# Float32 e of heads 2 to 7 in seven shared buffers, fewer whole chunks, v split in two passes, first loads in parts: an attention and feed-forward kernel

## The chip, the cores and the metric

The kernel runs on one core of a Trainium2 chip. The metric is the device time of one execution in microseconds (us). The engines are TensorE (PE in the rows, its weight loads PEld), VectorE (DVE), ScalarE (ACT), GpSimd (POOL) and SyncE (SP), which here only issues DMAs.

## The reference

Attention over 4 batches of 8 heads, with the queries averaged in pairs, and behind it one feed-forward block on the joined heads:

```
B, H, S, D = q.shape                      # 4, 8, 1152, 64
q_pool = q.reshape(B, H, S // 2, 2, D).mean(axis=3)
scores = np.matmul(q_pool, k.transpose(0, 1, 3, 2)) / np.sqrt(D)
scores = scores - np.max(scores, axis=-1, keepdims=True)
attn = np.exp(scores)
attn = attn / (np.sum(attn, axis=-1, keepdims=True) + 1e-09)
x = np.matmul(attn, v)                    # heads joined: 2304 tokens of 512
h = x @ w_in                              # 512 -> 1024
e = np.exp(h - np.max(h, axis=-1, keepdims=True))
solu = h * e / (np.sum(e, axis=-1, keepdims=True) + 1e-09)
out = layer_norm(solu) * g_ln @ w_out     # 1024 -> 512
```

## The kernel before, in words

A *head* g is one of the 32 (batch, head) combinations, a *pair* P two heads next to each other. A head has 576 averaged queries and 1152 keys, and the keys are taken in nine *chunks* j of 128, so that the kernel has 288 chunks, numbered s = 9g + j. For a chunk, TensorE multiplies the keys (stationary) by the queries into a PSUM bank, ScalarE writes the exponential, and TensorE multiplies e (stationary, 128 queries at a time) by the chunk's v of 64 columns and a column of ones, whose sum is the softmax's denominator. The maxima that are subtracted come from a coarser product of the same operands (`maxima`, VectorE's reductions of `mx`), one head ahead.

Float32 precision is reached in one of two ways. In a *split* chunk ScalarE writes e twice, as float16 (`eh`) and as float32 (`e32`, printed `e`), and GpSimd (`rest`, L1119) writes their difference, again float16, behind the first in the same buffer; v is split alike into `vhi` and `vlo`; TensorE then makes 12 float16 multiplications of 64 or 65 columns per chunk. In a *whole* chunk (`whole`, `values_whole`) e is written once, in float32, and TensorE multiplies it with the float32 `vx`, in four multiplications per chunk (five in heads 0 and 1). `EX` in the table `KP` says which chunks are whole: half of chunks 10 to 70. For e in float32 there are two buffers.

`pair(P)` loads k, q and v of a pair and prepares them. For v: a sum of absolute values (`am`), the scale `vs`, v times the scale in place (`v_mul`, on ScalarE in pairs with "B" in `VM`, on VectorE in the others), the float16 part (`v_hi`, ScalarE) and the difference (`v_lo`, GpSimd). Pair 0 has a path of its own: k is transposed by TensorE (`k_tr0`), copied by ScalarE to `w` (`k_hi0`) with VectorE making the rest (`k_lo0`), q likewise (`q_tr`, `q_hi`, `q_lo`) after its pairs were added (`pool_q`) and the sum copied beside itself (`dup_q`); a DMA copies k's upper part once more (`k_again`, L1072). Fifteen reductions of 384 columns give head 0's maxima, which are joined, transposed (`turn0`) and written as a row of `q2` (`shift0`) before its first scores.

The feed-forward weights come as 64 bit numbers in 16 parts, eight of `w_in` and eight of `w_out`. Each part is unpacked (`weight_part`: two `up` on ScalarE, two multiplications on TensorE, L547 and a maximum on VectorE) and later scaled and split in two float16 parts (`weight_split`: L605 on ScalarE, one multiplication, one VectorE pass). 18 token tiles of 128 follow (`tokens`), the first of them during head 9.

The order is made when the program is built. `add` notes each step with its engine, an estimated length and a due time in chunks, to which the table `OFF` adds a number of its own for each step; `Plan.run` goes through an estimated course in which each engine takes the ready step with the earliest due time whose buffers are free. What results is a fixed order on each engine; on the chip each instruction then waits for its semaphores. `warm` fills TensorE's gaps in the first chunks with transposes that nobody reads (L1554). `tag` says how many buffers of a name there are and which names share them: `zw1`, `zw2`, `zq1`, `zq2` (pair 0's k and q), `e` (the tokens'), `ln` and `lt` share seven.

Of the kernel before, what the change touches and what calls it, by code (L numbers as in the profile page):

```python
# [42 lines left out]
class Plan:  # L43
# [77 lines left out]
    def run(self):  # L121
# [85 lines left out]
        while events:  # L207
# [129 lines left out]
def attention_solu_moe(  # L337
# [47 lines left out]
    banks = {"np0": [(4,), (5,), (6,), (0,), (1,), (2,), (3,)], "cp0": [(0, 1), (2, 3)], "av": [(7,)], "opx": [(7,)], "tpp": [(0, 1), (2, 3)]}  # L385
# [5 lines left out]
    banks["tpf"] = [(0,), (1,), (2,), (3,)]  # L391
# [112 lines left out]
    for t in w2h:  # L504
        nc.gpsimd.memset(t[D:D + 1, :], ONE)
# [3 lines left out]
    for t in qb:  # L509
        nc.gpsimd.memset(t, 0.0)  # L510
# [414 lines left out]
    def maxima(g, at, span):  # L925
# [109 lines left out]
        if not P:  # L1035
            return finish(a)
# [549 lines left out]
```

## Time and profile before

| | |
|---|---|
| median of 3 runs | 625.68 us (624.82 to 627.17) |
| the profiled execution | 629.79 us, of which its span on the core 628.0 us |
| mean granted clock of TensorE | 0.991 |
| busy: PE, DVE, ACT, POOL | 601.0, 517.9, 502.5, 476.7 us |
| share of the span | 96%, 82%, 80%, 76% |

PE's busy time counts a matmul from its issue to its modelled end. The matmuls overlap, so a busy PE is not one at its peak; the distance between starts says what a matmul costs.

### The profile page before, as it was taken

To read this page: it belongs to the slowest core of one execution; us is meant where nothing else is said; L and a number is where in the kernel's file an instruction comes from. 1 tells how busy PE (TensorE), PEld (TensorE's weight loads), DVE (VectorE), ACT (ScalarE), POOL (GpSimd) and SP (SyncE) were. 2 spreads that over 40 slices of the span, in tenths; PEclk is the share of its full clock that TensorE was granted. 3 is DMA by queue.
4 is the path that set the end of the run, shared out by engine and by line. 5 is a ranking of instruction groups with operands and counts; after the bars stand their busy time and mean duration, and the time that the engine had idled before them with its cause. 6 is when DMAs were issued, how large, how long until landed. Compare 5 with 4: busy or idle time off the path is not lost. (4 is left out here: it accounts for less than half of the span.)

```text
span 628.0 us, 17132 instructions
## 1 busy us (share of the span) xinstructions
PE 601.0 (96%) x6637; PEld 376.3 (60%) x6637; DVE 517.9 (82%) x1112; ACT 502.5 (80%) x950; POOL 476.7 (76%) x487
## 2 busy tenths in 40 slices
PE   7999999999988799999999999999999999999997
PEld 7877767567645356656555565566556666654443
DVE  4999889988999979899998889797899795638731
ACT  4488797999889688998898889898789897946531
POOL 5198454758689899999999998899898999941110
PEclk8989999999899999999999999999999999999999
DMA  9466969577836659495949575958777644044712
GB/s 240 91 106 197 224 179 237 141 184 145 159 92 123 155 98 168 115 179 122 172 85 187 130 129 116 172 149 122 139 155 150 114 72 61 19 94 85 135 34 50
DMA packets 183374, 83.59 MB, mean 133 GB/s; under 512 B 168572, under 2 KB 168572, under 8 KB 183292
## 3 DMA queue, kind: packets, MB, share of 16 engines
q1 hardware_dynamic: 183212, 82.36, 62.9%
q8 instruction: 52, 0.85, 0.6%
q14 instruction: 30, 0.25, 0.1%
q10 hardware_dynamic: 80, 0.13, 0.1%
HBM read 36.70 MB, written 4.72 MB: 66 GB/s over the span
## 5 line engine op out<-in xcount | busy, mean ns | idle before, releaser
L1119 POOL TENSOR_TENSOR eh<-e,eh 128x512 f16<-128x512 f32 (+1 forms) x268 | 318.3, 1206 | 39.4 <-ACT e L1098 15.4
L955 DVE TENSOR_REDUCE mx<-bank 128x1 f32<-128x512 f32 (+1 forms) x300 | 188.0, 652 | 19.3 <-PE bank L457 18.7
L1098 ACT ACTIVATE eh<-bank 128x512 f16<-128x512 f32 (+3 forms) x267 | 159.3, 623 | 23.8 <-PE bank L457 22.9
L1098 ACT ACTIVATE e<-bank 128x512 f32<-128x512 f32 (+1 forms) x257 | 156.2, 617 | 22.3 <-POOL eh L1119 17.0
L457 PEld LDWEIGHTS <-eh 128*128 128x128 f16 x3112 | 132.9, 99 | 59.8 <-issue 5.3
L457 PE MATMUL bank<-q,w 128*128 128x64 f16 (+2 forms) x612 | 140.1, 291 | 7.5 <-ACT r L1109 2.3
L457 PE MATMUL bank<-vhi,eh 128*128 128x65 f16 x2070 | 144.6, 195 | 2.4 <-ACT eh L1098 1.2
L457 PE MATMUL bank<-q,w2h 65*128 65x512 f16 (+1 forms) x540 | 126.9, 287 | 0.0
L457 PE MATMUL bank<-wb,xt 128*128 128x512 f16 x432 | 111.9, 379 | 2.4 <-ACT eh L1098 1.4
L457 PE MATMUL bank<-wb,lt 128*128 128x512 f16 x432 | 112.8, 379 | 0.4 <-DVE e L1325 0.4
L457 PE MATMUL bank<-w,q 128*128 128x512 f16 (+2 forms) x390 | 107.1, 335 | 1.8 <-DVE mx L955 1.2
L457 PE MATMUL bank<-vlo,eh 128*128 128x64 f16 x1042 | 98.4, 195 | 0.0
L457 PEld LDWEIGHTS <-w2h 65*128 65x128 f16 x540 | 45.4, 98 | 36.2 <-issue 16.4
L457 PEld LDWEIGHTS <-xt 128*128 128x128 f16 x432 | 38.7, 98 | 39.3 <-issue 3.0
L457 PEld LDWEIGHTS <-w 128*128 128x128 f16 x540 | 47.3, 99 | 22.1 <-issue 1.5
L1125 POOL TENSOR_TENSOR er<-r,er 128x320 f16<-128x320 f32 (+1 forms) x60 | 51.5, 860 | 8.4 <-ACT r L1109 4.0
L457 PEld LDWEIGHTS <-lt 128*128 128x128 f16 x432 | 38.0, 98 | 33.2 <-issue 0.9
L897 POOL TENSOR_TENSOR vlo<-vx,vhi 128x1152 f16<-128x1152 f32 x16 | 39.5, 2467 | 19.8 <-ACT vhi L893 19.8
L1358 POOL TENSOR_TENSOR st<-st 128x1 f32<-128x1 f32 x54 | 14.3, 266 | 49.4 <-ACT junk L1345 44.3
L457 PEld LDWEIGHTS <-q 128*128 128x128 f16 x360 | 30.8, 99 | 16.2 <-issue 0.9
L457 PEld LDWEIGHTS bank<-vx,eh 128*128 128x128 f32 x256 | 32.0, 190 | 3.3 <-DVE x L1201 1.4
L1318 ACT ACTIVATE e<-bank,st,xs 128x512 f32<-128x512 f32 x36 | 27.9, 778 | 7.5 <-DVE st L1311 7.5
(130 smaller groups left out, 923.9 us busy)
## 6 DMA issues: line engine op xcount, KB each, us to landing
qt<-in_q_dram SPq DMA_DIRECT2D x16, 576.0 KB
kt<-in_k_dram SPq DMA_DIRECT2D x32, 288.0 KB
vx<-in_v_dram SPq DMA_DIRECT2D x32, 288.0 KB
out_dram<-o SPq DMA_DIRECT2D x35, 128.0 KB
khi<-w SPq DMA_DIRECT2D x30, 144.0 KB
w2h<-w SPq DMA_DIRECT2D x30, 144.0 KB
raw<-in_moe_w_in_dram SPq DMA_DIRECT2D x8, 511.6 KB
raw<-in_moe_w_out_dram SPq DMA_DIRECT2D x8, 511.6 KB
```

The lines of the kernel that those rows point to most:

```text
L457: nc.tensor.matmul(out=o, lhsT=a, rhs=b, start=first, stop=last, skip_group_check=True)
L897: nc.gpsimd.tensor_tensor(out=o, in0=t, in1=h, op=ALU.subtract)
L955: nc.vector.tensor_reduce(out=tl["mx", g][:, m, c:c + 1], in_=tl["nps", (g, m, c)], op=ALU.max, axis=AXX)
L1098: nc.scalar.activation(out=o if P else o.rearrange("p (f i) -> p f i", f=2), in_=i, func=ACTF.Exp, scale=esc)
L1119: eng.tensor_tensor(out=e[:, o:o + c.stop - c.start], in0=e32[:, c], in1=e[:, c], op=ALU.subtract)
L1125: eng.tensor_tensor(out=e[:, :, 1, :], in0=tl["r32", (g, u)][:, 0:len(RU[u]), :], in1=e[:, :, 0, :], op=ALU.subtract)
L1318: nc.scalar.activation(out=tl[E][:, f * 512:(f + 1) * 512], in_=tl[H_[f]], func=ACTF.Exp, bias=st(2), scale=xs[:, r, 3:4], accum_out=st(3 ...
L1358: nc.gpsimd.tensor_tensor(out=st(o), in0=st(a), in1=nhalf if b is None else st(b), op=op)
```

## The change

*e in float32.* `place` gives `e32` of heads 2 to 7 (`ZE`) to the seven shared buffers, which heads 0 and 1 have left and the tokens don't use yet. Later heads keep two.

*Fewer whole chunks.* `EX` of chunks 10 to 70 goes from 50 to 33 of 100: 31 whole chunks become 20, three in head 1 (before four) and 17 in heads 2 to 7 (before 27). Counted in the order: 45 float32 multiplications by `vx` fewer, 134 float16 ones with `eh` and `vhi` or `vlo` more, ten more exponentials `e` of 512 columns, nine more GpSimd differences `eh` of 512 (VectorE makes two more).

*v in two passes from pair 4* (`VN`). ScalarE scales and rounds in one pass (`v_hi`), VectorE scales and subtracts in one (`v_lo`, L471). `v_mul` and GpSimd's pass are gone there: 12 GpSimd passes fewer, 12 VectorE passes of the new kind for eight `v_mul`, four `v_mul` of ScalarE fewer.

*Pair 0.* k of head 0 and q are loaded in thirds, in turn, and each third is worked on by itself. The copy beside the sum is gone: `q_hi` writes the two halves of `q1` in two passes, and VectorE alone adds. `k_again` of heads 0 and 1 is no DMA any more but a second ScalarE copy from PSUM (`k_hi0b`). Head 0's maxima are closed in two parts, for the first 384 queries and the rest, and its scores, exponentials and PSUM banks are in halves of 288 queries (`tpq`). GpSimd's constant fills are steps of the plan, after the first needed ones, and ScalarE's table is loaded by a copy in the preamble. `k_hi` of pair 1 is made by GpSimd (`KH`).

*Times anew.* All of `OFF` is new, and in `KP` the due times of the weight parts (`W`) and of their splitting (`WS`), which are later. Counted by the exponentials `eh` ahead of them in ScalarE's order: of the 32 `up`, 6 stand in heads 0 and 1 as before, 16 in heads 2 to 7 (before 24), 10 in heads 8 to 11 (before 2). `w_out` is split beside chunks 93 to 103 (before 78 to 88). The first token's exponential stands at chunk 88 in both.

```diff
+        if k[0] == "e32":
+            a, z = KP["ZE"]
+            return ("ze32", *k[1:]) if a <= k[1][0] < z else k
...
-    tag(KP["ZB"], "zw1", "zw2", "zq1", "zq2", "e", "ln", "lt")
+    tag(KP["ZB"], "zw1", "zw2", "zq1", "zq2", "ze32", "e", "ln", "lt")
...
+            for i in range(3):
+                add("SP", DMA(kb / 3), -60 + i, lambda i=i: load_k0(0, i), [], [("kt", 0, (0, i))])
+                add("SP", DMA(2 * kb / 3), -59.5 + i, lambda i=i: load_q(i), [], [("qt", 0, i)])
+            add("SP", DMA(kb), -50, lambda: load_k0(1), [], [("kt", 0, 1)])
...
+        def k_hi0b(i, h):
+            o = tl["w2", h][0:D, i * PW:(i + 1) * PW]
+            nc.scalar.copy(out=o, in_=flat(tl["kps", (h, i, 0)]))
...
+            if P in KP["KH"]:
+                add("POOL", POOL(2 * SQ), at, lambda: k_hi(1), [KT, S_], [(*KN, 0)])
...
+            for s in range(2):
+                nc.scalar.copy(
+                    out=tl["q1", P][D * s:D * s + D, :, 3 * i:3 * i + 3, :],
+                    in_=tl["qps", (P, i)].rearrange("p t h i -> p h t i"),
+                )
...
+            nc.scalar.activation(out=o, in_=i, func=ACTF.Copy, scale=tl["vs", P][:, 3:4])
...
+            left(o, t, tl["vs", P][:, 3:4], h)
...
+            if P >= KP["VN"]:
+                add("ACT", ACT(2 * SQ, 1, 1), at_v + 4.5, v_hi, [V, S], [H_])
+                add("DVE", 1326, at_v + 5, v_lo, [V, S, H_], [("vlo", P, 0)], port=1)
+                return
...
+        def finish(ats):
+            for f, at in enumerate(ats):
+                add("DVE", 83, at, lambda f=f: all0(f), [("mx", g, m, c) for m in range(5)[MZ[f]] for c in range(3)], [("mz", 0, f)])
+                add("PE", TR(3 - f), at, lambda f=f: turn0(f), [("mz", 0, f)], [("cp0", (g, f))], kind="whole")
+                add("DVE", DVE((384, 192)[f]), at, lambda f=f: shift0(f), [("cp0", (g, f))], [("q2", 0, "cd"[f], g)])
```

In `KP`, `EX` goes from [[10, 71, 50], [42, 282, 0]] to [[10, 71, 33], [42, 282, 0]], `W` from [2, 4.44, 37.52, 4.7] to [5, 5.2, 61, 4.1], `WS` from [47, 70, 0.22] to [54, 96, 0.22]; `ZE` [2, 8], `VN` 4 and `KH` [1] are new.

Three places of the order follow. The first is the start of SP's queue, before (`kt` and `qt` are k and q, `vx` is v, `raw` a weight part, `w` pair 0's k):

```order
L640 DMA qt<-in_q_dram 128x1152
L637 DMA kt<-in_k_dram 128x576 x2
L648 DMA vx_80<-in_v_dram 128x9x64 x2
L632 DMA kt<-in_k_dram 128x576 x2
L528 DMA raw<-in_moe_w_in_dram 128x4093
```

And with the change:

```order
L644 DMA kt<-in_k_dram 128x192
L650 DMA qt<-in_q_dram 128x384
L644 DMA kt<-in_k_dram 128x192
L650 DMA qt<-in_q_dram 128x384
L644 DMA kt<-in_k_dram 128x192
L650 DMA qt<-in_q_dram 128x384
L644 DMA kt<-in_k_dram 128x576
```

One load of q and one of k became six small ones, k's first third at the head; v moved behind them, the first weight part far back.

The second place is the start of ScalarE's order before (`q` is the transposed q, `am` the sum over v):

```order
L670 ACT_TABLE_LOAD
L670 COPY qt<-qt 128x3x64
L751 CAST w_173<-bank 64x384
L784 CAST q_178<-bank 128x2x192
L751 CAST w_173<-bank 64x384 x2
L784 CAST q_178<-bank 128x2x192 x2
L537 ACTIVATE up<-raw,ebias 128x512 x2
L854 ACTIVATE vlo,am<-vx_80 128x1152
```

And with the change (`w_138` is head 0's k, `w_132` its second copy, `w_203` and `w_186` the same of head 1):

```order
L503 ACT_TABLE_LOAD
L503 COPY ebias<-nhalf 128x1
L746 CAST w_138<-bank 64x384
L750 CAST w_132<-bank 64x384
L746 CAST w_138<-bank 64x384
L750 CAST w_132<-bank 64x384
L795 CAST q_164<-bank 64x2x192 x2
L746 CAST w_138<-bank 64x384
L750 CAST w_132<-bank 64x384
L795 CAST q_164<-bank 64x2x192 x4
L746 CAST w_203<-bank 64x384
```

The copy of `qt`, which stood first and read what GpSimd adds, is gone; the six casts of head 0 became twelve, and the weight unpacking `up` no longer stands among them.

The third place is VectorE's order at v of pair 5, before (`wb` weights, `qb` q's lower part, `mx` maxima, `st` a token's maximum):

```order
L955 TENSOR_REDUCE mx<-bank 128x1
L889 TENSOR_SCALAR vx_81<-vx_81,vs 128x18x64
L467 SCALAR_TENSOR_TENSOR wb_69<-wb_69,ws_73,bank 128x512
L467 SCALAR_TENSOR_TENSOR qb_84<-qt,qs,qa 128x9x64
L1183 COPY low_2860<-bank 64x65
```

And with the change:

```order
L553 SCALAR_TENSOR_TENSOR wb_69<-raw,bank 128x512
L471 SCALAR_TENSOR_TENSOR vlo<-vx_81,vs,vhi_83 128x1152
L1358 TENSOR_REDUCE st<-bank 128x1
L471 SCALAR_TENSOR_TENSOR qb_84<-qt,qs,qa 128x9x64
L559 TENSOR_REDUCE wm_71<-wb_69 128x1
```

VectorE's scaling in place became its pass to `vlo`, and the weight work beside it is unpacking now, where it was splitting.

## Rows read from the trace of the kernel before

**Rows 1.** Busy time of each engine in six stretches; then PEclk, DMA share, GB/s

```profile
0.00:26.30 26.30, 22.61 (x161) 21.71 (x162) 15.91 (x36) 7.97 (x15) 10.02 (x24) 0.94 0.76 186
34.00:49.00 15.00, 14.85 (x177) 11.71 (x176) 14.05 (x28) 11.84 (x22) 14.26 (x19) 0.93 0.79 148
69.00:159.50 90.50, 87.23 (x971) 61.88 (x970) 81.80 (x181) 79.78 (x150) 56.16 (x49) 1.00 0.77 189
159.50:232.00 72.50, 63.26 (x795) 38.46 (x794) 66.64 (x141) 60.76 (x117) 60.76 (x58) 0.98 0.59 122
232.00:557.00 325.00, 320.96 (x3996) 192.75 (x3995) 277.86 (x598) 286.19 (x554) 308.26 (x292) 1.00 0.65 128
557.00:628.00 71.00, 66.42 (x315) 30.91 (x313) 36.48 (x84) 30.98 (x56) 8.51 (x30) 0.99 0.39 77
```

**Rows 2.** Timeline of the first 34 us: start, duration, engine, instructions; in brackets idle before

```profile
0.72 0.40 SPq L640 DMA_DIRECT2D qt<-in_q_dram  x1
...
4.66 0.63 DVE L666 TENSOR_TENSOR qt<-qt 128x192 f32<-128x192 f32 x2 [4.66 <-DMA qt<-in_q_dram]
...
6.63 1.21 DVE L500 TENSOR_SCALAR idb<-ident 128x128 bf16<-128x128 f32 x2
...
9.58 0.35 ACT L670 COPY qt<-qt 128x192 f32<-128x192 f32 x1 [3.59 <-POOL qt L666]
9.84 0.47 ACT L751 CAST w<-bank 64x384 fp32r<-64x384 f32 x1
...
10.34 0.55 DVE L460 TENSOR_TENSOR w<-bank,w 64x384 fp32r<-64x384 f32 x1 [2.49 <-ACT w L751]
...
15.67 7.06 DVE L1010 TENSOR_REDUCE mx<-bank 128x1 f32<-128x384 f32 x15 [1.50 <-PE bank L457]
...
26.34 1.32 PE L457 MATMUL bank<-q,w 128*128 128x288 f32 x8
...
33.78 3.31 POOL L1119 TENSOR_TENSOR eh<-e,eh 128x64 f16<-128x64 f32 x4
```

**Rows 3.** Groups by form, 69 to 159.5 us (heads 2 to 7): count, busy, mean ns

```profile
L1119 POOL TENSOR_TENSOR eh<-e,eh 128x512 f16<-128x512 f32 x29 | 34.8, 1211 | 18.5 <-ACT eh L1098 7.1 <-ACT e L1098 6.5 <-issue 3.0
L457 PE MATMUL bank<-vx,eh 128*128 128x65 f32 x216 | 28.1, 273 | 0.1
L1098 ACT ACTIVATE e<-bank 128x512 f32<-128x512 f32 x29 | 18.3, 659 | 0.0
L537 ACT ACTIVATE up<-raw,ebias 128x512 int16<-128x512 uint8 x11 | 8.8, 798 | 0.0
L553 DVE TENSOR_REDUCE wm<-wb 128x1 f32<-128x512 f32 x12 | 8.1, 676 | 0.0
L547 DVE SCALAR_TENSOR_TENSOR wb<-raw,bank 128x512 int32<-128x512 int32 x11 | 7.5, 684 | 3.1 <-PE bank L457 3.0
```

**Rows 4.** PE's timeline: a split chunk, a maxima product, a whole chunk (two records per multiplication)

```profile
102.66 0.19 PE L457 MATMUL bank<-vhi,eh 128*128 128x65 f16 x1
...
103.03 0.38 PE L457 MATMUL bank<-w,q 128*128 128x512 f16 x1
103.24 1.00 PE L457 MATMUL bank<-vx,eh 128*128 128x65 f32 x8
104.08 0.38 PE L457 MATMUL bank<-wb,id 128*128 128x512 f16 x1
```

**Rows 5.** Groups by form, whole run: v's passes and VectorE's k pass

```profile
L897 POOL TENSOR_TENSOR vlo<-vx,vhi 128x1152 f16<-128x1152 f32 x16 | 39.5, 2467 | 19.8 <-ACT vhi L893 19.8
L467 DVE SCALAR_TENSOR_TENSOR kn<-kt,qs,kn 128x1152 f16<-128x1152 f32 x15 | 26.7, 1781 | 3.9 <-ACT kn L727 3.8
L889 DVE TENSOR_SCALAR vx<-vx,vs 128x1152 f32<-128x1152 f32 x11 | 14.1, 1284 | 0.0
L887 ACT ACTIVATE vx<-vx,vs 128x1152 f32<-128x1152 f32 x5 | 6.3, 1266 | 2.3 <-DVE vs L874 2.3
```

**Rows 6.** Who waited for whom, 232 to 557 us: PE's longest and ACT's longest

```profile
PE bank L457 <- DVE mx L955: 1.5, 2, 0.9
...
ACT e L1098 <- POOL eh L1119: 13.9, 20, 2.3
```

More of the change, by code (lines that the diff above doesn't have):

```diff
@@ L497, in attention_solu_moe @@
     make_identity(nc, ident)
+    nc.gpsimd.memset(nhalf, -0.5)
+    nc.scalar.copy(out=ebias[:, 0:1], in_=nhalf)
     nc.vector.tensor_copy(out=id16, in_=ident)
@@ L710, in pair, with k_hi @@
             add("DVE", 75, a, q_inv, [("qs", P, 3), ("qs", P, 2)], [("qs", P, 1)])
-        else:
-            for i in range(3):
-                keys, c = [("qt", P, i)], slice(3 * i, 3 * i + 3)
-                if i in KP.get("QD", [0, 1]):
-                    add("DVE", DVE(192), at_q - 3, lambda c=c: pool_q(nc.vector, c), keys, keys, port=1)
-                    add("DVE", DVE(192, 1), at_q - 2, lambda c=c: dup_q(nc.vector.tensor_copy, c), keys, keys, port=1)
-                else:
-                    add("POOL", POOL(192) + 42, at_q - 3, lambda c=c: pool_q(nc.gpsimd, c), keys, keys)
-                    add("ACT", ACT(192, 0, 1), at_q - 2, lambda c=c: dup_q(nc.scalar.copy, c), keys, keys)
         def kn_part(t, i):
             return t.rearrange("p h j r d -> p (h j) r d")[:, :, i, :]
-        def k_hi():
+        def k_hi(pool=0):
             o = kn_part(new(("kn", P), [128, 2, NJ, 2, D], F16), 0)
+            if pool:
+                nc.gpsimd.tensor_scalar(out=o, in0=both(tl["kt", P]), scalar1=tl["qs", P][:, 2:3], scalar2=None, op0=ALU.mult)
+                return
             nc.scalar.activation(out=o, in_=both(tl["kt", P]), func=ACTF.Copy, scale=tl["qs", P][:, 2:3])
@@ L758, in prep_k0 @@
             ps, hi, lo = ("kps", (h, i, 0)), ("w1", h, i, 0), ("w1", h, i, 1)
-            add("PE", TR(3), at, lambda: k_tr0(i, h), [("kt", 0, h), *after], [ps], kind="whole")
+            src = ("kt", 0, 1) if h else ("kt", 0, (0, i))
+            add("PE", TR(3), at, lambda: k_tr0(i, h), [src, *after], [ps], kind="whole")
             add("ACT", ACT(PW), at, lambda: k_hi0(i, h), [ps], [hi])
             add("DVE", DVE(PW) + 4, at, lambda: k_lo0(i, h), [ps, hi], [lo])
+            if i == 0:
+                add("POOL", 1000, -39 + 30 * h, lambda: k_ones(h), [], [("w2", h, "one")])
+            add("ACT", ACT(PW), max(at, -7), lambda: k_hi0b(i, h), [ps], [("w2", h, "k", i)])
         def prep_k(at):
@@ L1045, in use_dve, with use_pool @@
         return any(a <= s < z and (s * b) % 100 < b for a, z, b in KP[key])
+    def use_pool(s):
+        return any(a <= s < z and (s * b + 50) % 100 < b for a, z, b in KP["PD"])
     RU = ((0, 1, 2, 3, 4), (5, 6, 7, 8))
@@ L1065, in w2 @@
             return w2h[plan.slot["w2", g]] if P else tl["w2", g]
-        def ones():
-            nc.gpsimd.memset(new(("w2", g), [D + 1, S], FR)[D:D + 1, :].bitcast(F32), 1.0)
         def k_again():
-            o, i = w2()[0:D, :], tl["w1", g][0:D, :]
-            nc.sync.dma_start(out=o if P else o.bitcast(F32), in_=i if P else i.bitcast(F32))
-        if not P:
-            add("POOL", 1000, -39, ones, [], [("w2", g, "one")])
-        add("SP", DMA(64 * S * (2 if P else 4), 200), at - OF[0], k_again, [("w1", g)], [("w2", g, "k")])
+            nc.sync.dma_start(out=w2()[0:D, :], in_=tl["w1", g][0:D, :])
+        if P:
+            add("SP", DMA(64 * S * 2, 200), at - OF[0], k_again, [("w1", g)], [("w2", g, "k")])
         def both_parts(ps, j, s, first, last):
@@ L1094, in product_rest, with expo @@
                 both_parts(ps[:, i, :], j, slice(MQ, SQ), True, True)
-        def expo(j, name, dtype):
-            o, i = new((name, (g, j)), [128, SQ * 4 // mybir.dt.size(dtype)], dtype)[:, 0:W], tl[tn(j), (g, j)]
+        def expo(j, name, dtype, f=None):
+            if f is not None:
+                if f == 0:
+                    new((name, (g, j)), [128, SQ * 4 // mybir.dt.size(dtype)], dtype)
+                nc.scalar.activation(
+                    out=tl[name, (g, j)][:, f * HALF:(f + 1) * HALF], in_=tl[tn(j), (g, (j, f))], func=ACTF.Exp, scale=esc
+                )
+                return
+            z = Plan.place((name, (g, j)))[0] == "ze32"
+            o, i = new((name, (g, j)), [128, S if z else SQ * 4 // mybir.dt.size(dtype)], dtype)[:, 0:W], tl[tn(j), (g, j)]
             nc.scalar.activation(
@@ L1206, in scores @@
         AVO, AV = KP["AV"], ("av", g)
-        V_ = [("vhi", P), ("vlo", P)]
+        V_ = [("vhi", P), ("vlo", P), ("vone", 0), ("vone", 1)]
         for j in range(NJ):
```

176 lines of the change are left out of this document (96 added, 80 removed).

## Prediction

> **What bounds the kernel now.** I read the stretches first, with each engine's busy time [rows 1]. From 232 to 557 us PE is busy 320.96 of 325 us, from 69 to 159.5 us 87.23 of 90.5; there every us of PE work taken out can be a us of time. Three stretches are otherwise. In the first 26.3 us PE's 161 matmuls are mostly the warming transposes: nothing useful runs until head 0's maxima are closed. From 34 to 49 us POOL is busy 14.26 of 15 us: it makes the differences of heads 0 and 1, all split. From 159.5 to 232 us PE has only 63.26 of 72.5 us and DVE leads with 66.64. The tail from 557 us is PE's alone.
>
> Then the timeline of the start [rows 2]. q, one load of 576 KB, is issued at 0.72 us and first used at 4.66. ACT's first copy waits until 9.58 us, 3.59 us of idle, because it reads a third of q that POOL adds behind its constant fills, and the casts of k stand behind it (9.84). So the 15 reductions begin at 15.67 and take 7.06 us, the scores begin at 26.34, and POOL's first difference at 33.78.
>
> **The start.** I walk through the new order with these durations. The first third of k (96 KB) lands somewhere between 0.72 + 3.94/6 = 1.4 us, if a load's time went by bytes alone, and 4.66; I take 2.7, nearer the bytes, and 3.4 for the first third of q. The Trainium skill (DMA: Bandwidth & Descriptors, section Anatomy of one DMA) speaks against small loads: each pays about 2 us whatever its size, by a fit for loads that GpSimd issues. By it, an estimate, the 96 KB land at 2.9 us, and the sum would be the same, unless the six pay one after the other; no row here prices a small load.
>
> ACT does six casts of 0.47 us before the first products can run, from 3.4 to 6.3 us. DVE has, until the first 384 maxima are closed, three additions (0.32 each), copies of the identity (some 1.9, from the 1.21 for two), nine lower parts at 0.55 and ten reductions at 0.47, with smaller ones about 13.5 us. From 3.5 us that ends at 17; with the transposes, the shift and two more reductions the first half of the scores starts at 19.5 us instead of 26.34 (-6.9), the second, whose maxima stand behind five further reductions, near 22.9 (-3.4). POOL needs both halves and starts at 24 instead of 33.78 (-9.8). But POOL binds heads 0 and 1, and it gets pair 1's k there, at most the 2.47 us of a pass over as many columns [rows 5] and at least none if it lies in a gap, and one more difference, 1.2 to 1.6. I take -9.8 + 2.4 + 1.4 = **-6**. The halves of 288 columns add ACT work that no row prices: 18 more passes than before, each pair of halves between one 0.659 pass of 512 and two, so 0 to 12 us, which I put at 4; ACT has 3 us free in the 15 from 34 to 49 and leaves 18 of the first 26.3 idle, so this is cover that is nearly used up. Bounds of the term -3.4 and -9.8.
>
> **Heads 2 to 7.** The twelve multiplications of a split chunk take 102.66 to 103.03, 0.37 us; those of a whole one 103.24 to 104.08, 0.84 [rows 4]. Ten whole chunks fewer (27 to 17; before, 216 records are 27 chunks [rows 3]) save PE 4.7 us. Four of the weight parts leave this stretch: eight PE multiplications at the 0.21 us between 103.03 and 103.24, 1.7 us. In exchange ACT writes ten more e at 0.659, 6.6 us, and loses eight `up` at 0.8, 6.4: even, at 79.8 us. DVE loses 4 x (0.676 + 0.684) = 5.4 us and gains pair 4's v pass; POOL gains 10 x 1.21 = 12.1 and has 56.16 of 90.5. With PE's load 6.4 us less and no other engine's greater, I take **-6.4**; if ACT becomes the bound, half of it; nothing lost. The seven buffers for e cost nothing and save nothing by themselves: ACT waits for POOL mainly after 232 us, 13.9 us in 20 waits [rows 6], where there are still two. Without them ten more differences would meet two buffers, and that wait would come here.
>
> **Heads 8 to 11**, 159.5 to 232 us. The four parts arrive here: PE 1.7, ACT 6.4, DVE 5.4. The splitting of `w_out` stays inside. v of two pairs: DVE's new pass reads two SBUF operands of 1152 columns, as its k pass does, 1.781 us, and replaces one of 1.284: +1.0; POOL -4.9 [rows 5]. DVE goes from 66.64 to 73, more than the 72.5 us that the stretch lasts now, and it cannot shrink. But half a stretch's waits were at single places (PE idles 9.2 us), and new times can put DVE work there. I take **+2.5**, between 0 and +6.
>
> **From 232 us.** Nine pairs: POOL loses 9 x 2.467 = 22.2 of its 308.26 us; DVE gains 9 x 1.781 - 6 x 1.284 = 8.3 on 277.86; ACT loses three `v_mul`, 3.8. PE idles 4 us here, and beside that waits inside its modelled busy time; ACT's 13.9 us behind POOL are shortened. I take **-3**, between +2 and -8. The tail's 71 us stay.
>
> **Sum.** -6 - 6.4 + 2.5 - 3 = -12.9. On the profiled execution, 628.0 us of span and 1.79 around it, 629.79 becomes 616.9; that run lies 0.66% above the median of 625.68, so **612.8** for a median.
>
> **Rivals.**
> *The middle stays full* (0.13). The start's 6 us come, but ACT and DVE, near 80 us in heads 2 to 7, do not let PE use its savings (-2), and DVE adds 4 in heads 8 to 11: -4, about 622. For it: DVE's 92% there. Against: neither load rises in heads 2 to 7.
> *The new times fill the gaps as well* (0.16). PE's idle time from 69 to 232 us is 12.5 us, and where it pauses the granted clock fell (0.93 from 34 to 49 us, 0.98 from 159.5). If half of it and half of ACT's 13.9 go, -12.9 - 8: about 604. For it: 1065 due times changed. Against: DVE has to carry it.
> *Slower: DVE stops POOL* (0.06). In each of the 12 new passes both engines want SBUF. If POOL stands still for the 1.78 us and the maxima behind the pass come late by as much, 11 pairs in heads 8 to 31 lose up to 2 x 1.78, 39 us; it decides the sign from 1.2 us per pair on, lost by PE itself. Half of the most, +19.6, gives 632. For it: VectorE's reductions of `mx` are what PE waits for longest (1.5 us in two waits) [rows 6]. Against: only 1.5 us in 325, and POOL is given 2.47 back each time. The Trainium skill (GPSIMD Engine Reference, section Key points) says that GpSimd shares its SBUF interfaces with VectorE and contends with instructions of two SBUF inputs; no row here separates the two, and by that rule POOL's relief is 0.7 us a pass, not 2.47.
> *No change* (0.05). The six loads land late, one after the other (six times something near q's 3.9 us), the reductions start where they did, and heads 2 to 7 are bound by ACT: 625. The parts would have to arrive after 12 us.
>
> **How the numbers follow.** The forecast has 0.60; its own range is 607 to 619, from the bounds of the terms taken half together. For 8 in 10 I add most of the case that fills the gaps and most of the full middle: 604 to 621. What a measurement of this kernel can tell from no change is about 0.5%: below 622.6 is faster, above 628.8 slower. Faster: 0.60 + 0.16 and 0.08 of the full middle, 0.84. Same: 0.05 of it and the 0.05, 0.10. Slower 0.06.
>
> **What would show it.** Right: first scores of 288 columns near 19.5 us, the first of POOL's `eh` near 24, the first `low` (end of head 0) some 5 us earlier than 49; 168 float32 records with `vx` where 248 were; heads 2 to 7 in about 84 us; `vlo` on VectorE at about 1.78 us each; from 232 us on POOL below 90% with PE still near 99%. Wrong: a DVE above 97% in heads 8 to 11 with PE waiting for `mx`; ACT idle behind POOL in heads 2 to 7; a first reduction after 12 us; a granted clock below 0.9 over the start, since fewer warming transposes (76 for 114) stand in it.

## The result and the profile after

The changed kernel takes 634.44 us (median of 9 runs, 628.78 to 636.55), the kernel before 626.32 us (9 runs, 621.96 to 628.71). The ratio is 1.0107, 95% interval 1.0070 to 1.0145: about 1% slower, where 2% faster was forecast. The profiled execution took 630.42 us, its span 628.6 us, the mean granted clock 0.978 (before 0.991).

The stretches of the changed kernel, columns as in [rows 1]:

```profile
0.00:26.30 26.30, 22.93 (x167) 19.45 (x167) 21.01 (x50) 17.19 (x38) 13.90 (x28) 1.00 0.63 175
34.00:49.00 15.00, 13.75 (x102) 10.21 (x102) 11.55 (x22) 9.89 (x22) 13.84 (x18) 0.77 0.86 195
69.00:159.50 90.50, 82.31 (x971) 56.84 (x971) 77.89 (x174) 77.93 (x145) 56.28 (x51) 0.94 0.67 163
159.50:232.00 72.50, 65.14 (x766) 38.73 (x765) 65.86 (x143) 65.32 (x125) 54.90 (x53) 0.93 0.68 156
232.00:557.00 325.00, 321.12 (x4017) 195.09 (x4015) 275.23 (x602) 284.18 (x551) 293.06 (x286) 1.00 0.64 127
```

Against [rows 1], PE is busy 4.9 us less from 69 to 159.5 us, and no other engine notably more. That looks like the forecast. But the clock column reads 0.77, 0.94 and 0.93 where it read 0.93, 1.00 and 0.98. Busy time at a lower clock is less work, so the stretches have to be cut at the same work. I cut them where a head ends, at the end of the copy `low` in VectorE's timeline:

| end of head, us | before | after | before, pauses filled | after, pauses filled |
|---|---|---|---|---|
| 1 | 69.04 | 65.26 | 66.74 | 65.18 |
| 7 | 159.43 | 158.03 | 158.28 | 155.97 |
| 11 | 232.03 | 235.20 | 224.65 | 230.98 |
| 31 | 557.03 | 557.26 | 548.17 | 553.05 |
| span | 628.0 | 628.6 | 619.1 | 624.4 |

(The two right columns are of the experiments below.) Heads 0 and 1 gain 3.8 us, heads 2 to 7 lose 2.4 (90.4 becomes 92.8), heads 8 to 11 lose 4.6, heads 12 to 31 gain 2.9. The profiled execution of before lies 3.5 us above its median and that of after 4 us below its own, so the columns are read for where the time goes, and the timed runs for how much.

The start, in the timeline of the changed kernel:

```profile
3.68 0.36 DVE L784 TENSOR_TENSOR qt<-qt 128x192 f32<-128x192 f32 x1 [3.68 <-DMA qt<-in_q_dram]
5.06 0.47 ACT L746 CAST w<-bank 64x384 fp32r<-64x384 f32 x1 [2.86 <-PE bank L741]
9.01 1.02 DVE L1038 TENSOR_REDUCE mx<-bank 128x1 f32<-128x384 f32 x2
19.82 0.52 PE L461 MATMUL bank<-q,w 128*128 128x288 f32 x2
24.22 4.20 POOL L1158 TENSOR_TENSOR eh<-e,eh 128x64 f16<-128x64 f32 x6 [0.52 <-ACT e L1131]
28.41 3.20 POOL L720 TENSOR_SCALAR kn<-kt,qs 128x1152 f16<-128x1152 f32 x1
34.37 1.07 PE L461 MATMUL bank<-up,idb 128*128 128x512 bf16 x4 [1.72 <-DVE mx L980]
39.64 2.37 POOL L916 TENSOR_TENSOR vlo<-vx,vhi 128x1152 f16<-128x1152 f32 x1
```

Against [rows 2], the first scores come 6.5 us earlier (26.34) and POOL's first difference 9.6 us earlier (33.78), as forecast. Then PE pauses 1.72 us. What follows such a pause is seen in windows laid on the pauses and behind them (columns as in [rows 1]; PE busy 0.00 is a pause):

```profile
32.65:34.37 1.72, 0.00 (x1) 0.00 (x1) 1.69 (x3) 0.93 (x2) 1.72 (x2) 1.00 0.54 82
35.50:42.30 6.80, 6.75 (x55) 5.64 (x51) 3.85 (x8) 5.08 (x13) 6.80 (x8) 0.50 0.77 149
43.00:49.00 6.00, 5.17 (x39) 3.42 (x39) 5.54 (x11) 4.34 (x8) 4.84 (x9) 1.00 1.01 261
87.37:89.45 2.08, 0.00 (x0) 0.00 (x0) 2.08 (x3) 0.81 (x2) 0.22 (x1) 1.00 0.39 120
90.60:93.40 2.80, 2.80 (x26) 1.73 (x24) 1.19 (x2) 2.06 (x6) 0.00 (x0) 0.50 0.87 178
139.03:140.30 1.27, 0.00 (x0) 0.00 (x0) 1.23 (x4) 1.27 (x3) 0.88 (x1) 1.00 1.04 298
141.50:148.40 6.90, 6.90 (x51) 4.55 (x51) 4.81 (x12) 4.65 (x11) 4.27 (x5) 0.52 0.45 150
194.30:199.80 5.50, 3.13 (x15) 1.17 (x16) 5.23 (x16) 4.74 (x10) 5.44 (x7) 0.65 0.67 142
200.00:206.50 6.50, 6.42 (x91) 4.98 (x90) 4.39 (x11) 4.27 (x7) 5.13 (x3) 0.53 0.86 141
```

After each of these pauses TensorE runs at half clock, the 1.2 GHz level, for 3 to 10 us, and then again at 2.4 GHz. The last of them, from 195.9 us, is an exception: it began behind two waits of 0.62 us, ahead of the longest wait there (1.14 us). From 28 to 232 us there are four such stretches, some 27 us long; summed in windows of 1 us, the clock lost (one less the granted clock) is 13.6 us over the span. In the kernel before it is 5.8 us, of which 1.7 fall on warming transposes at 12 to 15 us.

One of the places, in PE's and VectorE's timelines of the changed kernel:

```profile
86.99 1.81 DVE L471 SCALAR_TENSOR_TENSOR kn<-kt,qs,kn 128x1152 f16<-128x1152 f32 x1
...
89.45 0.38 PE L461 MATMUL bank<-w,q 128*128 128x512 f16 x1 [2.09 <-DVE mx L980]
...
91.27 0.26 PE L461 MATMUL bank<-q,w 128*128 128x64 f16 x1
91.39 0.24 PE L461 MATMUL bank<-q,w 128*128 128x64 f16 x1
```

VectorE's pass for k stands ahead of five reductions, PE waits for the first of them, and 2 us later its pairs of small scores follow each other at 0.12 us. The Trainium skill (TensorE: Matmul & The Clock Gate, section What's actually happening) has the idle engine throttled and activity releasing it; the trace agrees in kind, with 0.50 behind pauses of 1.72 and 2.08 us.

Heads 2 to 7 by form, as in [rows 3]:

```profile
L1158 POOL TENSOR_TENSOR eh<-e,eh 128x512 f16<-128x512 f32 x34 | 39.7, 1179 | 27.5 <-ACT eh L1137 16.2 <-DMA zq<-q 4.6 <-issue 3.4
L1137 ACT ACTIVATE e<-bank 128x512 f32<-128x512 f32 x35 | 20.9, 615 | 1.6 <-PE bank L461 1.6
L461 PE MATMUL bank<-vx,eh 128*128 128x65 f32 x136 | 18.6, 281 | 0.0
L543 ACT ACTIVATE up<-raw,ebias 128x512 int16<-128x512 uint8 x8 | 6.1, 759 | 0.0
```

136 records are 17 whole chunks, as forecast; POOL's idle time ahead of its differences went from 18.5 to 27.5 us, waiting for ACT's `eh`. So the work went where it should, and the engines wait more for each other.

### The profile page after: what moved, and what is told of

Read it like the earlier page. It is cut to its first block, busy times and chain, and to the rows that moved or that the text cites. A ratio compares the mean times of both kernels' runs of the same rounds, so it can differ in the third digit from the quotient of the medians.

```text
span 628.6 us, 17188 instructions
## 1 busy us (share of the span) xinstructions
PE 596.5 (95%) x6643; PEld 370.0 (59%) x6643; DVE 512.0 (81%) x1120; ACT 509.3 (81%) x982; POOL 463.3 (74%) x485
## 4 chain that ended last, share of the span: by engine, by line
PE 68%; DVE 19%; ACT 6%; issue 3%; DMA 2%; SPq 1%; POOL 0%; DVEq 0%; ACTq 0%; POOLq 0%
PE bank L461 66%; DVE mx L980 5%; DVE kn L471 2%; DVE qb L471 2%; PE bank L1604 1%; DVE e L1375 1%; DVE st L1358 1%; ACT eh L1137 1%; ACT e L1137 1%; DMA vx<-in_v_dram 1%; DMA w2h<-w 1%; DVE vlo L471 1%; ACT up L543 1%; DVE wb L471 1%; DVE x L1240 1%
## 5 line engine op out<-in xcount | busy, mean ns | idle before, releaser
L1158 POOL TENSOR_TENSOR eh<-e,eh 128x512 f16<-128x512 f32 (+1 forms) x278 | 333.5, 1216 | 69.0 <-ACT eh L1137 26.6
L1137 ACT ACTIVATE eh<-bank 128x512 f16<-128x512 f32 (+3 forms) x257 | 152.2, 611 | 28.5 <-PE bank L461 27.5
L461 PEld LDWEIGHTS <-eh 128*128 128x128 f16 x3246 | 137.4, 99 | 57.6 <-issue 11.2
L461 PE MATMUL bank<-vhi,eh 128*128 128x65 f16 x2159 | 148.5, 196 | 3.2 <-DVE x L1240 3.0
L461 PE MATMUL bank<-q,w 128*128 128x64 f16 (+2 forms) x612 | 143.8, 296 | 5.9 <-ACT e L1137 3.6
L461 PE MATMUL bank<-q,w2h 65*128 65x512 f16 (+1 forms) x540 | 129.4, 292 | 0.2 <-DMA q<-c 0.2
L461 PE MATMUL bank<-wb,lt 128*128 128x512 f16 x432 | 109.8, 379 | 0.0
L461 PE MATMUL bank<-vlo,eh 128*128 128x64 f16 x1087 | 103.3, 195 | 0.0
L1408 POOL TENSOR_TENSOR st<-st 128x1 f32<-128x1 f32 x54 | 13.9, 257 | 55.4 <-ACT junk L1395 53.7
L1375 DVE SCALAR_TENSOR_TENSOR e<-bank,xs,e 128x512 f32<-128x512 f32 x36 | 26.3, 740 | 6.1 <-ACT e L1368 6.0
L1148 ACT ACTIVATE er<-bank 128x320 f16<-128x320 f32 (+1 forms) x60 | 25.6, 427 | 6.9 <-PE bank L461 6.6
```

Of the source, the lines that this page charges most:

```text
L461: nc.tensor.matmul(out=o, lhsT=a, rhs=b, start=first, stop=last, skip_group_check=True)
L1137: nc.scalar.activation(out=o if P else o.rearrange("p (f i) -> p f i", f=2), in_=i, func=ACTF.Exp, scale=esc)
L1148: nc.scalar.activation(out=o, in_=tl[rn(u), (g, u)], func=ACTF.Exp, scale=esc)
L1158: eng.tensor_tensor(out=e[:, o:o + c.stop - c.start], in0=e32[:, c], in1=e[:, c], op=ALU.subtract)
L1375: nc.vector.scalar_tensor_tensor(out=tl[E][:, s], in0=tl[H_[f]], scalar=xs[:, r, 3:4], in1=tl[E][:, s], op0=ALU.mult, op1=ALU.mult, accum_ ...
L1408: nc.gpsimd.tensor_tensor(out=st(o), in0=st(a), in1=nhalf if b is None else st(b), op=op)
```

## The experiments

I had two explanations. *The clock*: PE's freed time becomes pauses, and each pause is paid twice, by itself and by half clock behind it. *Starvation*: steps that are late on ScalarE, VectorE or GpSimd cost the time, and the clock only shows it. To tell them apart, transposes that nobody reads were put into the pauses of the finished order (`t` is the planned start of a step, `busy[e]` the end of the one before it), so that every engine keeps its order:

```diff
+            if e == "PE" and FILL[0] < t < FILL[1] and t - busy[e] > FILL[2]:
+                ...                       # i: a free bank, since done_at[i]
+                    for _ in range(int((t - max(busy[e], done_at[i])) / 110)):
+                        extra.append((t - 0.5, lambda i=i: self.warm(*i)))
```

**Filled change.** `FILL = [24000, 236000, 300]`: 206 transposes.

> The changed kernel with its orders on all engines untouched, but with transposes that nobody reads put into TensorE's order wherever the plan sees it idle for more than 0.3 us between 24 and 236 us (about 230 of them, 0.11 us each). Theory 1, the clock: the pauses themselves cost little, but after each TensorE runs at the 1.2 GHz level for 4 to 11 us, 27 us in all in the profiled execution (sum of lost clock 13.6 us, of which 5.8 in the kernel before). With the pauses filled the granted clock should be 0.985 or more over the span, the half-speed time from 28 to 232 us should fall below 10 us, and the time from about 634 to 624-628 us. Theory 2, starvation: TensorE waits because ScalarE, VectorE and GpSimd come later; filling changes no wait, so the time stays at 632-637 us or grows, whatever the clock does.

625.6 us (before on that chip 628.2), ratio 0.9957 (0.9943 to 0.9971). The granted clock of the profiled run:

```profile
core 0: 624.4 us, clock 0.999
```

Work was added, none was taken away, and 1.5% of the time went (1.0107 to 0.9957): the slowdown against the kernel before is the clock's. At the place shown above the transposes stand in the pause, and the pairs of scores behind it follow at 0.06 us:

```profile
87.68 2.38 PE L1615 MATMUL bank<-ident 128*128 128x128 f32 x20
...
91.19 0.19 PE L472 MATMUL bank<-q,w 128*128 128x64 f16 x1
91.25 0.19 PE L472 MATMUL bank<-q,w 128*128 128x64 f16 x1
```

**Kernel before, filled** in the same way (64 transposes).

> The kernel before, its orders untouched, with the same transposes put wherever its plan sees TensorE idle for more than 0.3 us between 24 and 236 us. It gives the change's worth at full clock: filled change against filled before. Theory 1: the kernel before loses 4 to 5 us by half-speed time in useful work, so 623-625.5 us at a granted clock of 0.997 or more, and the filled change (625.6) is then no better: what is missing of the forecast's 12.9 us beside the clock lies in waits. If all terms of the forecast had come and only the clock was missed, the filled kernel before would be near 634 us, which is above the kernel before itself, so this cannot hold whole; at 628 (no gain by filling) the change without its clock is worth 2.6 us.

623.8 us (before 627.2), ratio 0.9950 (0.9927 to 0.9974). So with its pauses filled the change is worth nothing: 0.9957 against 0.9950. The timed runs agree, though less sharply. A line through time against lost clock, (1 - granted clock) x time, of 135 runs of the kernel before rises 1.00 us per us and meets zero lost clock at 621.7 us (correlation 0.69); that of the nine runs of the change rises 0.77 and ends at 621.3. Those nine lie at 10 to 19 us of lost clock, so the end of their line is uncertain by some 2 us, and charged with every us of it they would lie at 617.9 in the mean. Nor are the transposes free, and the filled change has three times as many. So at full clock the change is worth between nothing and some 4 us. What is missing of the 12.9 us lies elsewhere than in the clock. The two profiled executions that follow differ by 5.3 us, and the medians of the two kernels by 1.8, since that of before was the fastest of its twelve; so these stretches show the change some 3.5 us too slow in all. PE's busy time of heads 2 to 7 and of heads 8 to 11 in the two filled kernels, first in all and then for the transposes alone, before:

```profile
66.74:158.28 91.54, 88.37 (x987) 64.16 (x989) 82.46 (x180) 80.38 (x151) 57.27 (x50) 1.00 0.74 186
158.28:224.65 66.37, 63.18 (x820) 39.73 (x818) 62.14 (x142) 60.00 (x116) 61.06 (x57) 1.00 0.61 130
66.74:158.28 91.54, 2.59 (x18) 2.21 (x19) 1.00 0.74 186
158.28:224.65 66.37, 3.35 (x26) 2.61 (x24) 1.00 0.61 130
```

And with the change:

```profile
65.18:155.97 90.79, 89.33 (x1093) 65.69 (x1091) 80.42 (x178) 78.16 (x149) 58.34 (x54) 1.00 0.68 165
155.97:230.98 75.01, 71.19 (x857) 45.06 (x856) 69.08 (x152) 70.67 (x136) 60.29 (x59) 1.00 0.72 159
65.18:155.97 90.79, 11.13 (x87) 9.91 (x88) 1.00 0.68 165
155.97:230.98 75.01, 7.89 (x60) 6.56 (x59) 1.00 0.72 159
```

In heads 2 to 7 PE's own work falls from 88.37 - 2.59 = 85.8 to 89.33 - 11.13 = 78.2 us, by 7.6; the heads get 0.75 us shorter. The rest stands as transposes in pauses. In heads 8 to 11 its work grows by 3.5 us, ACT's by 10.7 and DVE's by 6.9, and the heads get 8.6 us longer. Part of ACT's growth is no new work. The ends of heads are marks on VectorE, and ScalarE's lead over them differs: counted by each chunk's first exponential in the traces, in the kernel before it is 5 chunks ahead at the end of head 7 and 2 at the end of head 11, in the changed one 3 and 5. So more of its exponentials fall between these two marks, in the filled kernels before and after:

```profile
L1109 ACT ACTIVATE e<-bank 128x512 f32<-128x512 f32 x34 | 20.4, 604 | 3.2 <-POOL eh L1130 3.0
L1148 ACT ACTIVATE e<-bank 128x512 f32<-128x512 f32 x40 | 25.0, 632 | 1.8 <-PE bank L472 0.8 <-POOL eh L1169 0.8
```

**The parts, planned anew.** Three kernels change one entry of `KP`; the plan then makes its order again, with due times that were found for other steps.

```diff
+ ex_50:              'EX': [[10, 71, 50], [42, 282, 0]]      in the change
+ v_one_pass:         'VN': 16, old due times of v            in the change
+ before_fewer_whole: 'EX': [[10, 71, 34], [42, 282, 0]]      in the kernel before
```

> The changed kernel with half of chunks 10 to 70 whole again (31 where the change has 20), all else as changed; its order is planned anew. If the fewer whole chunks are worth the 0.47 us each that the prediction reckoned, the time is 634 + 4.7 = 639 us. Theory 1, clock: TensorE is the bound in heads 2 to 7 again, pauses less, its clock rises to about 0.985 and the time is 628-633 us in spite of the added work. Theory 2, starvation by the ten more exponentials and the nine more GpSimd differences: 627-631 us, with fewer waits of TensorE for ACT, and the clock not decisive.

> The changed kernel with v of pairs 4 to 15 prepared as before (VectorE or ScalarE scales, ScalarE rounds, GpSimd subtracts), with the due times of these steps as they were before. Theory 3, the two passes on VectorE are what makes maxima late: the time falls to 627-630 us and the loss of 4.6 us in heads 8 to 11 goes. Theory 1: the time stays at 634, within 3 us, and heads 12 to 30 lose the 2.9 us that the change gained there.

> The kernel before with 34 of 100 of chunks 10 to 70 whole where it has 50 (18 in heads 2 to 7 where the change has 17), all else as before, two buffers for e in float32. By the prediction's price: nine chunks of 0.47 us less, 626 - 4.2 = 622 us, or less of it where ScalarE then waits for GpSimd with two buffers. Theory 1: TensorE pauses more often in heads 2 to 7, its granted clock over the span falls from 0.991 to 0.985 or less, and the time is 624-630 us. Theory 2: the extra e and differences alone make it slower, 628-633 us, with ACT waiting for POOL.

665.97, 684.45 and 659.43 us (ratios 1.056, 1.091 and 1.051). All miss what was expected by 25 us or more, in the same direction, whether a part is taken out or put in. They price no part: each set of due times gave a good order only with the steps that it was found for. In v_one_pass PE is busy 76.23 of the 90.5 us from 69 us on, at a granted clock of 0.83. From here on orders were kept.

**Less or more work in a kept order.** In the first, `values_whole` leaves out two of four multiplications; in the second, four transposes are put ahead of a split chunk's multiplications (they start the running sum of their bank anew, so these sums are not whole); the third cuts the exponential `e32` and its difference to 64 columns. All take the same ten chunks.

```diff
+                if NJ * g + j in CUT and m in (1, 2):      # before_less_pe
+                    continue
+                extra.extend((t - 0.5, lambda i=i: self.warm(i, 384)) for _ in range(4))   # filled_more_pe
+            if name == "e32" and NJ * g + j in CUT:        # filled_less_e
+                o, i = o[:, 0:64], i[:, 0:64]
```

> The kernel before with two of the four float32 multiplications left out in ten of its 27 whole chunks of heads 2 to 7 (0.42 us each, 4.2 us of TensorE's work; those chunks' sums are left incomplete), all orders untouched and nothing added on any engine. My prediction's premise, every us of TensorE's work taken out there is a us of time: 628 - 4.2 = 624 us. Theory 1: TensorE pauses instead, its clock falls once or twice more (span mean below 0.988), and the time is 627-631 us. A third way, TensorE not the bound and its clock unmoved: 627-628 us.

624.68 us, ratio 0.9972 (0.9944 to 1.0001): 1.8 us by the ratio for 4.2 us of work, at a clock of 0.991 in the mean. My premise is at most half true in the order of before (the interval reaches from no gain to 3.5 us), and the clock did not fall there as theory 1 expected. So less work on TensorE, in an order left as it was, did not make pauses that cost the clock.

> The filled change with four more transposes that nobody reads in each of ten split chunks of heads 2 to 7 that were whole before (40 x 0.11 = 4.4 us, about what the change took out). If TensorE is the bound of heads 2 to 7: 625.6 + 4.4 = 630 us. If these heads are set by the exponentials of ScalarE and by waits, the added work goes into pauses: 625.6 to 627 us.

629.64 us, ratio 1.0041 (1.0019 to 1.0062): 4 to 5 us more than the filled change. For the order without transposes this tells little, since they already fill the pauses that could have taken the work. It does show that transposes are not free there: heads 2 to 7 took 93.8 us for 90.8.

> The filled change with the ten added exponentials in float32 and their ten differences cut to 64 of 512 columns in the same ten chunks (about 0.45 us less on ScalarE and 0.9 us less on GpSimd each; the lower part of e is left out there), orders untouched. If the work that the fewer whole chunks put on ScalarE and GpSimd is what holds heads 2 to 7: 625.6 - 4.5 = 621 us or down to 618. If the places of the waits hold them and not the load (a weight part that lands late, maxima that end late): 625 us, within 1.

626.43 us, ratio 1.0009: no gain. The ten added exponentials and differences are not what holds heads 2 to 7, as far as a filled order can show it.

**Fewer transposes, k on ScalarE, half of the v passes, less weight work.**

```diff
-                    for _ in range(int((t - max(busy[e], done_at[i])) / 110)):
+                    for _ in range(int((t - max(busy[e], done_at[i])) / 220)):     # fill_half
-                add("POOL", POOL(2 * SQ), at, lambda: k_hi(1), ...
+                add("POOL", POOL(2 * SQ), at, lambda: k_hi(0), ...                 # khi_on_scalar
-            left(o, t, tl["vs", P][:, 3:4], h)
+            left(o[:, 0:NJ], t[:, 0:NJ], tl["vs", P][:, 3:4], h[:, 0:NJ])          # v_lo_half
+        N = 64 if m and n % 8 > 2 else WN   # less_weights: columns of up, join and top
```

In less_weights VectorE's step that joins the parts keeps its 512 columns and reads the raw part a second time in place of the bank.

> The filled change with half as many transposes in each pause (95 in place of 206, about 5 us less of them). If what holds the clock is that TensorE does not pause long, and the transposes themselves cost nothing: 625 us, within 1, at a clock of 0.995 or more. If the transposes stand in the way where the pause on the chip is shorter than in the plan: up to 5 us faster than the filled change, 621-624 us. If half of them is not enough: the clock falls to 0.985 or less and the time goes to 629 us or more.

626.58 us, ratio 0.9990 (0.9966 to 1.0015), clock 0.992 to 0.999: half of the transposes nearly hold the clock, and gain nothing.

> The filled change with the upper part of pair 1's k made by ScalarE at the same place of the program, as before the change, in place of GpSimd's pass of 3.20 us; all orders else untouched. The prediction took this pass as 2.47 us on the engine that binds heads 0 and 1. If GpSimd binds there, head 1 ends 2 to 3 us earlier and the time is 622.5-624 us. If ScalarE has no room there (some 1.3 us), it is 625 us or above.

625.92 us; head 1 ends at 65.31 us (filled 65.18). GpSimd's 3.20 us pass alone does not set the end of head 1. The run cannot tell whether GpSimd doesn't bind there or ScalarE, which got the pass, has no room for it.

> The filled change with VectorE's new pass of v (pairs 4 to 15) over 576 of 1152 columns (the lower part of v of every second head is left out there); all orders untouched. Theory 3, these passes hold maxima up: 12 x 0.75 us less on VectorE, of which two stand in heads 8 to 11: 621-623 us. If they lie in cover: 625.6 us, within 1.

625.83 us, no gain: the passes lie in cover. Theory 3 falls, and with it the rival of the prediction that VectorE stops GpSimd, whose cost would have halved.

> The filled change with the work of the last five weight parts, which stand in heads 8 to 11 since the change, cut down: ScalarE's unpacking and VectorE's maximum over 64 of 512 columns, TensorE's multiplications likewise (the upper halves of these parts of w_out are left out). About 5.5 us less on ScalarE and 2.6 us on VectorE. Theory 4, the moved weight parts are what heads 8 to 11 lost (75.0 us against 66.4 of the filled kernel before): these heads take 70 us or less and the time is 620-622 us. If other waits set them: 625 us, within 1.5.

628.4 us: heads 8 to 11 took 78.3 us, 3.4 us of lost clock in it, so about 75 as before, with ACT busy 67.2 us where it was 70.7. Theory 4 falls.

**One pause, and the weights without their loads.** fill_start has transposes up to 60 us only; no_w_out_load adds 64 columns for all parts of `w_out`.

```diff
-FILL = [24000, 236000, 300]
+FILL = [24000, 60000, 300]          # both
+        N = 64 if m else WN         # no_w_out_load: columns of fetch, up, join, product and top
```

> The changed kernel with the transposes put into its planned pauses between 24 and 60 us only (60 in place of 206). The half-speed time from 35 to 42 us goes (3.4 us of lost clock), that from 90, 141 and 195 us stays (10 us). Theory 1, each pause costs by the clock behind it: about a third of the 9.4 us that the full filling gave, 630-632 us, at a clock of 0.980-0.986. Theory 2 (waits alone, the clock being a symptom): 634 us.

630.22 us, ratio 1.0041 (1.0017 to 1.0064), clock 0.978 to 0.992: 0.66% less than the change, where a third of its filling's 1.5% was expected.

> As fill_start, and the eight parts of w_out (from about 130 us on) cut to 64 of 512 columns in their load (64 in place of 512 KB), ScalarE's unpacking, TensorE's multiplications and VectorE's maximum; a fill with zeros and a short product stand for VectorE's product (these columns of w_out are left out). Theory 5, the moved weight parts hold heads 6 to 11 by their loads and work, and the pauses at 140 and 195 us are theirs: heads 8 to 11 take 70 us or less where the changed kernel has 77, TensorE does not fall to the 1.2 GHz level there, and the time is 619-623 us. Theory 6, the fixed order holds these heads at other places: 628 us or more, with the pauses at 157, 174 and 195 us still there.

626.37 us, ratio 0.9985 (0.9963 to 1.0006), between the two theories and 0.56% less than fill_start. Heads 6 and 7 got 2 us shorter, but heads 8 to 11 took 75.2 us against 75.8, with no engine busy more than 66.9 us of them. PE's longest waits near their middle are the same, in length and place. In fill_start:

```profile
197.64 0.38 PE L472 MATMUL bank<-q,w 128*128 128x512 f16 x1 [0.87 <-ACT e L1148]
200.21 0.59 PE L472 MATMUL bank<-q,w 128*128 128x512 f16 x1 [1.14 <-ACT e L1148]
```

And without the loads and the work:

```profile
192.42 0.38 PE L472 MATMUL bank<-q,w 128*128 128x512 f16 x1 [0.87 <-ACT e L1151]
194.99 0.59 PE L472 MATMUL bank<-q,w 128*128 128x512 f16 x1 [1.14 <-ACT e L1151]
```

The load is not the cause in heads 8 to 11 (theory 5 falls there). Heads 2 to 7 of this execution kept full clock without any transposes behind 60 us:

```profile
64.45:154.75 90.30, 80.45 (x1005) 55.87 (x1003) 78.65 (x180) 76.72 (x149) 59.22 (x55) 1.00 0.68 146
```

So they take the 90.4 us of the kernel before at full clock too, and it isn't the transposes that hide the forecast's 6.4. That left the order of single steps.

**The order at the pauses.** A list moves steps ahead of others in the finished order; one_place has its first line, three_places all, and three_places_filled the 206 transposes as well.

```diff
+AHEAD = [
+    (('DVE', 'kn', 3, 1), [('DVE', 'mx', 5, 1, 1), ('DVE', 'mx', 5, 2, 0), ('DVE', 'mx', 5, 2, 1)]),
+    (('DVE', 'xn', 0, 1), [('DVE', 'wm', 1, 10), ('DVE', 'wm', 1, 8)]),
+    (('ACT', 'ln', 0, 0), [('ACT', 'e32', (10, 4), 0)]),
+    (('ACT', 'wo', 0, 8), [('ACT', 'e32', (10, 5), 0)]),
+]
```

> As fill_start, and at one place VectorE's order changed: three reductions of head 5's maxima stand ahead of the pass for k of pair 3 (1.81 us) that made TensorE pause 2.1 us at 87 us. Theory 6, the fixed order makes the pauses and each costs twice, by itself and by the clock behind it: the pause falls below 0.5 us, the 1.2 GHz level behind it (90 to 99 us) goes, heads 2 to 7 get 3 to 5 us shorter and the time goes from 630 to 625-628 us. If the place is held by something else as well: 629-631 us.

629.27 us, ratio 1.0048 (1.0017 to 1.0079): no faster than fill_start. Yet the pause at 87 us is gone, and head 3 ends at 91.54 us where it ended at 96.26. 2.1 us of pause and the clock behind it were worth 4.7 us at that place. The pass for k now comes later, and 8 us on PE waits for what a DMA makes of it:

```profile
96.25 0.81 PE L482 MATMUL bank<-w,q 128*128 128x512 f16 x3 [1.56 <-DMA w<-kn]
```

Of the 4.7 us, 3.8 are left at the end of head 7, 1.3 at the end of head 11 and 1.0 at the end; 1.7 of what went in heads 8 to 11 is half clock that fill_start's execution didn't have there.

> As one_place, with two more places: two maxima of weight parts behind head 9's shift on VectorE (pause of 1.45 us at 157 us), and two exponentials of head 10 ahead of a pass for the tokens and a weight part on ScalarE (pause of 1.14 us at 199 us). Theory 6: heads 8 to 11 get 2 to 4 us shorter as well, 622-626 us, at a clock of 0.988 or more. If heads 8 to 11 are held by load: no gain beyond one_place.

628.06 us, ratio 1.0046 (1.0020 to 1.0072). The wait of 1.45 us for VectorE near 159 us became one of 0.92 us for ScalarE's `e`; heads 8 to 11 took 77.0 us (the profiled execution, 632.36 us, was the slowest of its twelve).

> The order of three_places with the transposes of the filled change in all its planned pauses (the same 206). Theory 6: at most as fast as three_places where that holds its clock, and faster where it does not: 621-624 us, below both kernels. If the transposes now stand where no pause is left: 625 us, no better than the filled change.

627.07 us, ratio 1.0014 (0.9991 to 1.0037): no better than the filled change.

## Why the prediction was wrong, step by step

**The start** (-6): right as far as it was dated. First scores 19.82 us for 19.5, GpSimd's first difference 24.22 for 24, first reductions 9.01. The term was mis-sized behind that: head 0 ends 1.4 us earlier, not 5, head 1 3.8 us, and at full clock 1.6 us. GpSimd's 18 differences of head 0 ended at 44.8 us, 3.3 us before the 48.1 of the kernel before, though they began 9.6 us earlier. Three steps now stand among them that stood outside before: the pass for k (3.20 us, not 2.47 at most), a copy for q (0.94) and v's difference (2.37 us at 39.64), which in the kernel before came behind them:

```profile
48.06 2.38 POOL L897 TENSOR_TENSOR vlo<-vx,vhi 128x1152 f16<-128x1152 f32 x1
```

Of the three the sum had the first alone. The pause of 1.72 us and the half clock from 35.5 to 42.3 us stand in these heads too; how much each cost is not shown, and khi_on_scalar, which took the first away, moved head 1's end by 0.1 us. The halves of 288 columns took 0.444 us each, so 18 pairs cost some 4 us more than 18 whole passes of 0.650, as put.

**Heads 2 to 7** (-6.4, "nothing lost"): this step failed. The price of the work was about right (7.6 us of PE's time gone at full clock for 6.4, 17 whole chunks; the `vx` records are 160, not the 168 that were given as a sign). But "every us of PE work taken out there can be a us of time" was read from PE's share, 87.23 of 90.5 us. A busy engine is a price list only if what it waits for comes earlier as well, and here it did not: in heads 2 to 7 of the two profiled executions PE's longer waits grew from 2.8 us to 6.7 in all, those on `mx` from 0.3 and those on `up` from none:

```profile
PE bank L461 <- DVE mx L980: 2.6, 3, 2.1
PE bank L461 <- ACT up L543: 1.6, 2, 1.3
```

206 transposes went into the planned pauses of the changed order where 64 went into those of before. 0.75 us of the 6.4 came in the filled pair, and with the clock a loss of 2.4. Whether the pauses come from the smaller work or from the new due times is not separated: with work taken out of the old order (before_less_pe) the clock did not fall.

**The clock** had no term. I watched it at the start, where it stayed at 1.00, and the rival with the new times even read [rows 1]'s 0.93 and 0.98 as the cost of pauses; the trace bears it out for the first, with a pause of 1.20 us at 31.4 us and half clock from 32.6 to 36.1. But I let pauses only shrink. The clock made the sign of the result: filled, the change goes from 1.0107 to 0.9957, the kernel before to 0.9950.

**Heads 8 to 11** (+2.5, 0 to +6): mis-sized. It measured +4.6 in the profiled pair and +8.6 in the filled pair; all kernels with the changed order take 75 to 78 us there, those with the order of before 66 to 73. DVE's added work was about as counted (6.9 us for 6.4), ACT's was not (10.7 for 6.4), in part because more of its exponentials fall between these two marks. Neither the v passes nor the unpacking nor the loads hold it. Which steps do stays open; two of them, moved, gave nothing.

**From 232 us** (-3): -2.9 in the profiled pair, but -1.4 in the filled pair, and that it fits so well is in part luck: the three executions with the order of before took 322.6, 323.5 and 325.0 us there, those of the changed order 322 to 323. GpSimd is busy 293.06 of 325 us (before 308.26), and ACT's wait behind it fell (beside [rows 6]):

```profile
ACT e L1137 <- POOL eh L1158: 8.0, 20, 0.6
```

That this made the gain is not shown; ACT's wait for PE grew from 11.8 to 16.3 us in the same stretch.

The new pass of v takes 1.57 us, not 1.78, and GpSimd keeps four of its 16 (beside [rows 5]):

```profile
L471 DVE SCALAR_TENSOR_TENSOR vlo<-vx,vs,vhi 128x1152 f16<-128x1152 f32 x12 | 18.8, 1570 | 1.0 <-ACT vhi L911 1.0
L916 POOL TENSOR_TENSOR vlo<-vx,vhi 128x1152 f16<-128x1152 f32 x4 | 9.5, 2378 | 10.7 <-ACT vhi L909 10.7
```

**The rival that came** was none of the four. "The middle stays full" had the gain stop, but by the load of ACT and DVE; cutting that load gave nothing. In the rival with the new times, half of 12.5 and half of 13.9 make 13.2 us, not the 8 that its 604 was made with.

## What to carry to other kernels

Where several engines stand near 90%, the busiest one's share is no price list: work taken from it is time only if what it waits for also comes earlier, and a wait removed at one place came back in part 8 us later at the next. Ask of every saving on TensorE whether it leaves pauses like those above, of 1.3 to 2.1 us; one of 2.1 us cost 4.7 us at its place, and transposes that nobody reads, put into the pauses, gave more than they cost. And change one part in a kept order: with a plan made anew each part "cost" 30 us or more, and told nothing. Compare stretches in more than one execution: heads 8 to 11 took 66 to 73 us in three of the same order.

## What the runs showed of the hardware

In the changed kernel a pause of 1.27 us between dense matmuls was followed by 7 us at half clock, while one of 1.45 us passed without:

```profile
157.54:158.99 1.45, 0.01 (x1) 0.00 (x0) 1.39 (x6) 1.45 (x4) 1.36 (x3) 1.00 1.23 126
159.10:165.00 5.90, 5.54 (x89) 3.48 (x88) 4.09 (x9) 5.85 (x13) 5.21 (x5) 1.00 0.54 117
```

Nor is the same pause followed by the same stretch in every execution: the 2.1 us at 87 us by 3 us of half clock in the changed kernel, by none in no_w_out_load (its row from 64.45 us above), and by 10 us in fill_start:

```profile
86.60:88.60 2.00, 0.00 (x0) 0.00 (x0) 2.00 (x3) 0.95 (x2) 0.18 (x1) 1.00 0.35 107
88.70:99.50 10.80, 10.36 (x69) 6.59 (x70) 5.77 (x14) 5.40 (x11) 3.02 (x3) 0.53 0.89 154
```

So the time of a kernel with pauses spreads: the nine runs of the change lie between 628.78 us at a clock of 0.984 and 636.55 at 0.970, the twelve of the filled change between 624.36 and 626.91.
